# Attention and two feed-forward layers in one kernel: a planner's cost figures, 285 ranks and the place of three steps are changed

## The chip, the cores and the metric

One core of one Trainium2 chip. The metric is the device time of one execution in microseconds (us), median of three runs.

## The reference

Inputs: q, k, v of 4 batches x 8 heads x 576 tokens x 64, a scalar tau, and two pairs of float32 weights (512 x 2048 and 2048 x 512).

```python
scores = q @ k.T / sqrt(64)                        # per batch and head
scores = where(scores >= scores.max(-1) - tau, scores, -1e9)
attn   = exp(scores - scores.max(-1))
x      = (attn / (attn.sum(-1) + 1e-9)) @ v        # -> 2304 tokens x 512
h = x @ moe_w_in;   g = h * sigmoid(1.702 * h);     x = g @ moe_w_out
h = x @ moe2_w_in;  g = h * tanh(softplus(h));      out = g @ moe2_w_out
```

## The kernel before, in words

**Attention.** Heads are taken in pairs (16 of them). A pair of heads gives four full query tiles of 128 rows, and every second pair a mixed tile of the rows left over: 72 tiles in all, called groups in the code. For each group TensorE (PE) makes the scores of two heads into four PSUM banks (`qk`, L591). VectorE (DVE) scales them and takes the row minimum of the negated scores (L614), GpSimd (POOL) adds tau to that minimum (L618), ScalarE (ACT) takes the exponential (L621), DVE masks it and sums the rows (L624). PE then turns the result in 128x128 blocks (`turn`, L660 and L665), ACT copies the turned blocks out (L680), PE multiplies by v (`product`, L703, and `product_mix`, L728) and ACT copies that product out (L712, L735). Only the four banks `sc` hold scores, so the scores of a group wait for the two L614 of the group before.

**Feed-forward layers.** Each layer goes over 3 blocks of 768 tokens and 8 pairs of 128 hidden columns, so there are 24 steps n per layer and 48 in all. `hidden(n)` multiplies by w_in in a 7-product Strassen form (42 matmuls of 384 columns, L829) with ACT and DVE combining and activating (L843, L846, L851), and `out1`/`out2` multiply by w_out (L904, L907, L949). Every float32 matmul is made of three passes over a rounded operand and its remainder (L444/L445, L466/L467, L519/L520).

**Weights.** They arrive as 64-bit words. `conv_w` turns 1024 columns of them into float32: two ACT instructions (L377, L379), two DVE tensor_scalar (L383, L386), one integer addition on POOL (L389), one DVE instruction (L391). `stage` converts the two halves of one pair and stores them to a DRAM tensor `w_d`. `weights(n)` converts on the spot (`stage`, ring `sv` of four tiles), or loads what is in `w_d` back (L427), and then splits it into the operands of step n (L444 to L467). For n of 1 and 2 the operands' tiles share memory with tiles of the attention and open only when that has let go of them. The tuple `EARLY = (1, 2, 3)` says that pairs 0, 1 and 2 are converted during the attention: pair 0 by `weights(0)`, pairs 1 and 2 by `stage` through a ring `sg` of two tiles, to be read back from `w_d` later. `load_xs(0)` brings the attention's output in for block 0 (L494, L520, L524).

**What sets the order.** Nothing is ordered by hand. `Order.add` records every step with its engine, a duration in us, the keys that it reads and writes, and a rank. `Order.run` plays the steps through a list scheduler: an engine that is free takes the ready step of lowest rank and never idles while one is ready; the order that comes out is the order in which the instructions are issued, and on the chip each engine then keeps to it. Attention steps have ranks about equal to their group's number (0 to 71), `load_xs(0)` has 80, all weight work and all feed-forward steps have 5,000 or more. So weight work goes where the plan has an engine free. The durations are formulas (`t_mm`, `t_dve`, `t_act`, `t_tt`), the delay from one engine's end to another's start is the table `LAT`, and steps marked `port` (two-input or fast DVE steps and the POOL steps) may not overlap one another in the plan.

Of the kernel before, what the change touches and what calls it, by code (L numbers as in the profile page):

```python
# [32 lines left out]
FI = 20  # L33
HALF = 384
NHS = 4
SLACK = 0.0
AHEAD = 2
NSS = 6
EARLY = (1, 2, 3)
XR = 80  # L40
S0 = 8
S1 = 2
SR = 0.0
WR = 0.0


class Order:
# [7 lines left out]

    LAT = {
        "PE": {"PE": 0.0, "ACT": 0.27, "DVE": 0.2, "POOL": 0.27, "SP": 0.2},
        "DVE": {"PE": 0.26, "ACT": 0.13, "DVE": 0.13, "POOL": 0.16, "SP": 0.2},
        "ACT": {"PE": 0.22, "ACT": 0.08, "DVE": 0.15, "POOL": 0.16, "SP": 0.2},
        "POOL": {"PE": 0.22, "ACT": 0.08, "DVE": 0.15, "POOL": 0.1, "SP": 0.2},  # L60
        "SP": {"PE": 0.95, "ACT": 0.95, "DVE": 0.95, "POOL": 0.95, "SP": 0.95},
# [2 lines left out]
    def __init__(self):  # L64
        self.ops = []
        self.writer = {}
        self.readers = {}
        self.fill = None
        self.port = set()
        self.mode = {}  # L70

    def add(self, eng, dur, fn, r=(), w=(), rank=0.0, deps=(), nbytes=None, port=False, steps=1, mode=0):
        n = len(self.ops)
        if mode:
            self.mode[n] = mode
        if port:
            self.port.add(n)
        before = set(deps)
        for key in r:
            if key in self.writer:  # L80
                before.add(self.writer[key])
        for key in w:
            if key in self.writer:
                before.add(self.writer[key])
            before.update(self.readers.get(key, ()))
        for key in r:
            self.readers.setdefault(key, []).append(n)
        for key in w:
            self.writer[key] = n
            self.readers[key] = []  # L90
        before.discard(n)
        self.ops.append((eng, dur, fn, before, rank, nbytes, steps))
        return n

    def run(self):
        n_ops = len(self.ops)
        after = [[] for _ in range(n_ops)]
        left = [len(o[3]) for o in self.ops]
        ready = [0.0] * n_ops
        for i, o in enumerate(self.ops):  # L100
            for d in o[3]:
                after[d].append(i)
        engines = sorted({o[0] for o in self.ops})
        free = dict.fromkeys(engines, 0.0)
        future = {e: [] for e in engines}
        now = {e: [] for e in engines}
        for i, o in enumerate(self.ops):
            if not left[i]:
                heapq.heappush(future[o[0]], (0.0, i))
        free["SP"] = 1.0  # L110
        self.last = 0.0
        wire = 0.0
        order = []
        port, done = 0.0, 0
        held, took = 0, {}
        while done < n_ops:
            best = None
            for e in engines:
                if now[e]:
                    t = free[e]  # L120
                elif future[e]:
                    t = max(free[e], future[e][0][0])
                else:
                    continue
                if best is None or t < best[0]:
                    best = (t, e)
            t, e = best
            while future[e] and future[e][0][0] <= t:
                i = heapq.heappop(future[e])[1]
                heapq.heappush(now[e], (self.ops[i][4], i))  # L130
            aside = []
            i = None
            if e == "PE":
                item = min(now[e], key=lambda x: (x[0] + KEEP * (self.mode.get(x[1], 0) != held), x[1]))
                now[e].remove(item)
                heapq.heapify(now[e])
                i = item[1]
            while i is None and now[e]:
                item = heapq.heappop(now[e])
                if item[1] in self.port and port > t + 1e-6:  # L140
                    aside.append(item)
                    continue
                i = item[1]
                break
            for item in aside:
                heapq.heappush(now[e], item)
            if i is None:
                free[e] = port
                continue
            done += 1  # L150
            _, dur, _, _, _, nbytes, _ = self.ops[i]
            if e == "PE" and self.mode.get(i, 0) != held:
                held = self.mode.get(i, 0)
                dur += TURN
            took[i] = dur
            free[e] = end = t + dur
            if i in self.port:
                port = end
            self.last = max(self.last, end)
            if nbytes is not None:  # L160
                wire = end = max(wire, end + DMA_US) + nbytes / DMA_RATE
            order.append((t, i))
            for a in after[i]:
                lat = self.LAT[e][self.ops[a][0]] if dur or nbytes else 0.0
                ready[a] = max(ready[a], end + lat + SLACK)
                left[a] -= 1
                if not left[a]:
                    heapq.heappush(future[self.ops[a][0]], (ready[a], a))
        self.order = order = sorted(order)
        if self.fill is not None:  # L170
            eng, until, dur, fn = self.fill
            at, gaps = 1.2, []
            for t, i in order:
                if i == until:
                    break
                if self.ops[i][0] == eng:
                    n = int((t - at - FG) / dur) if gaps else FI
                    if n > 0:
                        gaps.append((at, i, n))
                    at = t + took[i]  # L180
            order = sorted([(t, i, 0) for t, i in order] + gaps)
        else:
            order = [(t, i, 0) for t, i in order]
        events = []
        for t, i, n in order:
            _, _, fn, *_, steps = self.ops[i]
            dur = took[i]
            if n:
                events.append((t, len(events), self.fill[3], n))
            elif steps == 1:  # L190
                events.append((t, len(events), fn))
            else:
                for k in range(steps):
                    events.append((t + dur * (k + 1) / steps, len(events), next_of, i, k))
        running = {}
        for _, _, fn, *args in sorted(events, key=lambda x: x[:2]):
            if fn is next_of:
                i, k = args
                if k == 0:
                    running[i] = self.ops[i][2]()  # L200
                next(running[i], None)
            else:
                fn(*args)
# [7 lines left out]
def attention_then_two_ffn_kernel(  # L211
# [86 lines left out]
    def t_mm(n, k=1):  # L298
        return k * (max(n, 256) * 0.4167e-3 + 0.0125)
# [8 lines left out]
        return 0.16 + n * 0.97e-3  # L308

    def t_tt(n):  # L310
        return 0.15 + n * 2.1e-3

    def dma(fn, nbytes, r=(), w=(), rank=0.0, deps=(), dur=0.47):
        return add("SP", dur, fn, r, w, rank, deps, nbytes)
# [253 lines left out]
    def qk(tl, rank):  # L568
# [6 lines left out]
        def mm():  # L575
# [18 lines left out]
                yield  # L594

        add("PE", 1.02, mm, [h[2] for h in kqt], [("sc", i) for i in range(4)], rank,
            steps=4 if full else 10, mode=1)
        return [(sc[i][:, :, 0:SH], [("sc", 2 * i), ("sc", 2 * i + 1)]) for i in range(2)]

    def softmax_a(sums, ksum, col, rank, bank, pair, i):  # L600
# [87 lines left out]
    def product(tl, rank):  # L688
# [4 lines left out]
        pn = [p for p, _ in turned[b, hp]]  # L693
        i = avn[0] % 2
        avn[0] += 1
        av, kav = tb[3][:, i * 256:i * 256 + 256], ("tb", 3, i)

        def mm(cs):
            for c in cs:
# [15 lines left out]
    def product_mix(b, hp, i, pn, rank):  # L715

        _, vr, _, kvr = head[b, hp]
        av, kav = tb[2][:, 256 + 64 * i:320 + 64 * i], ("tb", 2, 1 + i)

        def mm():  # L720
            for c in range(5):
# [75 lines left out]
        reopen("g", i, [("p", i)] + ([("pmt", i)] if i < 2 else []))  # L797
    for i in range(3):
        reopen("x2", i, [("vr", i)])
    open_hb = add("SP", 0.0, open_h, deps=scored, rank=-10.0)  # L800
    load_xs(0, XR)
    for n, at in enumerate(EARLY):
# [12 lines left out]
    def hidden(n, rank):  # L815
# [16 lines left out]
                    yield  # L832

        def product(p, dst, kd, start):
            i = add("PE", t_mm(HALF, 6) + 0.03, lambda: mm(p, dst, start),
                    [("xq", p), ("win", n % 3, p)], [kd], rank + PO[p] / 8, [open_hb] if n == 0 else [], steps=6)
            firsts.setdefault(n, i)

        def h(i, j, x, kx, y=None, ky=None):
            ht, kh = hs[i]  # L840
            cs = slice(j * HALF, (j + 1) * HALF)
            if y is not None:
                add("DVE", t_dve(HALF), lambda: nc.vector.tensor_tensor(ht[:, cs], x(), y, ALU.add),  # L843
                    [kx, ky], [kh + (j,)], rank - 4.0)
            add("ACT", t_act(HALF),
                lambda: nc.scalar.activation(ht[:, cs], x() if y is None else ht[:, cs], fn),  # L846
                [kx] if y is None else [], [kh + (j,)], rank - 4.0)

# [86 lines left out]
    def out2(n, rank):  # L935
# [6 lines left out]
        for q, (i, ts) in enumerate(order):  # L942
            g, kg = units[i]

            def mm(i=i, ts=ts, g=g):
# [7 lines left out]
                        )  # L953
                        yield

            add("PE", 3 * len(ts) * t_mm(512), mm, kg + [("wout", n % 3)], [ka2[t] for t in ts],
                rank + (q + 0.5) / len(order), steps=3 * len(ts))
        if k == KP - 1:
            for t in range(6):
# [82 lines left out]
```

## Time and profile before

| what | value |
|---|---|
| median of 3 runs | 1037.9 us (1037.72 to 1038.08) |
| profiled execution | 1037.93 us, of which the span of instructions is 1036.2 us |
| PE, DVE, ACT, POOL busy | 1020.9, 832.7, 659.7, 168.7 us |
| attention, first score to last product | about 6 to 279 us |
| first and second feed-forward layer | about 270 to 655 us, 655 to 1036 us |

The span is the time from the first instruction to the last; 1.7 us of the execution lie around it. A busy PE is one with a matmul under way, and since matmuls are pipelined and long, PE reads as nearly full even where its matmuls start late. DVE and ACT busy times can be taken as they stand. "Idle before" names what ended an engine's idle time. Times are from the start of the span.

### The profile page before, as it was taken

What the parts mean: (1) busy time and instruction counts of PE and PEld (TensorE: products, weight loads), DVE (VectorE), ACT (ScalarE), POOL (GpSimd) and SP (SyncE); (2) the same over time, 40 slices, a digit from 0 to 9 for tenths busy, and PEclk for the clock granted to TensorE, in tenths of its full rate; (3) what the DMA queues carried; (4) which work ended last, traced back from release to release, by engine and by line L of the source; (5) the groups of instructions that cost most, each with busy time, mean ns of one, the idle gap of its engine ahead of it and who ended that gap; (6) DMA issues with size and microseconds to landing.
All of it is one profiled execution on the core that took longest, in us unless ns stands there. A gap on an engine that the chain in (4) does not pass through costs nothing.

```text
span 1036.2 us, 17403 instructions
## 1 busy us (share of the span) xinstructions
PE 1020.9 (99%) x6348; PEld 866.9 (84%) x6348; DVE 832.7 (80%) x1642; ACT 659.7 (64%) x1261; POOL 168.7 (16%) x182
## 2 busy tenths in 40 slices
PE   9999999999999999999999999999999999999998
PEld 6666666666698999999999999988889889889887
DVE  7999999999877889888798888865688665975633
ACT  5988787887866668666687667744464444544421
POOL 2543543333122210111211112000000000000000
PEclk9999999999999999999999999999999999999999
DMA  5434556443145536756376534612125112142001
GB/s 196 126 143 160 175 188 196 131 131 94 45 131 182 180 122 236 250 170 222 134 264 219 203 107 164 199 64 79 63 90 173 62 61 82 46 138 82 21 1 61
DMA packets 55942, 139.62 MB, mean 135 GB/s; under 512 B 8496, under 2 KB 18736, under 8 KB 55856
## 3 DMA queue, kind: packets, MB, share of 16 engines
q1 hardware_dynamic: 55856, 138.51, 39.8%
q8 instruction: 49, 0.80, 0.3%
q14 instruction: 37, 0.30, 0.1%
HBM read 107.48 MB, written 31.01 MB: 134 GB/s over the span
## 4 chain that ended last, share of the span: by engine, by line
PE 80%; ACT 8%; DVE 7%; DMA 2%; issue 1%; POOL 1%; SPq 0%; DVEq 0%; ACTq 0%; POOLq 0%
PE h L829 27%; PE tb L949 13%; PE tb L904 8%; PE sc L591 7%; PE tb L703 7%; PE h L949 6%; PE tb L665 6%; PE h L907 4%; DMA sv<-w_d 1%; PE tb L728 1%; DVE hs L843 1%; DVE xq L520 1%; ACT wout1a L680 1%; ACT sr L379 1%; ACT hs L846 1%
## 5 line engine op out<-in xcount | busy, mean ns | idle before, releaser
L843 DVE TENSOR_TENSOR hs<-h,u 128x384 f32<-128x384 f32 x144 | 79.7, 553 | 78.1 <-ACT u L851 54.5
L829 PE MATMUL h<-xq,win 128*128 128x384 f32 x672 | 131.5, 336 | 2.4 <-ACT u L851 2.2
L829 PE MATMUL h<-xq,win2b 128*128 128x384 f32 x672 | 131.7, 335 | 1.9 <-DVE hs L843 1.5
L829 PE MATMUL h<-xq,win1b 128*128 128x384 f32 x672 | 131.4, 335 | 0.0
L846 ACT ACTIVATE hs<-hs 128x384 f32<-128x384 f32 x144 | 75.9, 527 | 78.9 <-DVE hs L843 77.6
L829 PEld LDWEIGHTS h<-xq,win2b 128*128 128x128 f32 x672 | 116.0, 188 | 8.4 <-DVE hs L843 1.8
L829 PEld LDWEIGHTS h<-xq,win 128*128 128x128 f32 x672 | 115.6, 188 | 8.4 <-ACT u L851 2.9
L829 PEld LDWEIGHTS h<-xq,win1b 128*128 128x128 f32 x672 | 115.9, 188 | 5.6
L851 ACT COPY u<-h 128x384 f32<-128x384 f32 x144 | 68.6, 476 | 78.5 <-PE h L829 78.1
L614 DVE TENSOR_SCALAR_CACHE_REDUCE win2a<-sc,nqsc 128x576 f32<-128x576 f32 x144 | 111.4, 810 | 4.4 <-PE sc L591 4.0
L618 POOL TENSOR_SCALAR nm<-nm,tau_p 128x1 f32<-128x1 f32 x144 | 86.1, 599 | 159.6 <-DVE win2a L614 158.3
L591 PE MATMUL sc<-win1a 64*128 64x288 f32 (+3 forms) x672 | 91.8, 414 | 0.8 <-DVE win2a L614 0.7
L389 POOL TENSOR_TENSOR sg<-sg,sr 128x1024 uint32<-128x1024 uint32 x20 | 51.9, 2594 | 226.7 <-DVE sg L386 225.2
L449 DVE TENSOR_TENSOR sv<-sv 128x256 f32<-128x256 f32 x192 | 84.1, 442 | 0.2
L591 PEld LDWEIGHTS sc<-win1a 64*128 64x128 f32 (+1 forms) x672 | 52.2, 173 | 28.3 <-DVE win2a L614 9.4
L444 ACT CAST win2b<-sv 128x256 fp32r<-128x256 f32 (+1 forms) x96 | 41.9, 442 | 33.6 <-DVE sv L449 28.1
L444 ACT CAST win<-sv 128x256 fp32r<-128x256 f32 (+1 forms) x96 | 42.2, 448 | 30.2 <-DVE sv L449 26.6
L444 ACT CAST win1b<-sv 128x256 fp32r<-128x256 f32 (+1 forms) x96 | 42.1, 444 | 29.4 <-DVE sv L449 23.6
L445 DVE TENSOR_TENSOR win<-sv,win 128x256 fp32r<-128x256 f32 (+1 forms) x96 | 48.9, 512 | 9.7 <-ACT win L444 9.5
L445 DVE TENSOR_TENSOR win2b<-sv,win2b 128x256 fp32r<-128x256 f32 (+1 forms) x96 | 45.9, 479 | 13.5 <-ACT win2b L444 13.4
L445 DVE TENSOR_TENSOR win1b<-sv,win1b 128x256 fp32r<-128x256 f32 (+1 forms) x96 | 44.1, 462 | 11.9 <-ACT win1b L444 11.7
L680 ACT COPY wout1a<-tb 128x512 f32<-128x512 f32 x72 | 40.7, 598 | 11.6 <-PE tb L665 11.3
(242 smaller groups left out, 2283.7 us busy)
## 6 DMA issues: line engine op xcount, KB each, us to landing
sv<-w_d SPq DMA_DIRECT2D x84, 512.0 KB
sr<-in_w_in SPq DMA_DIRECT2D x16, 1024.0 KB
sr<-in_w_out SPq DMA_DIRECT2D x32, 512.0 KB
w_d<-sg SPq DMA_DIRECT2D x20, 512.0 KB
win1a<-in_kq SPq DMA_DIRECT2D x16, 576.0 KB
xr<-x_d SPq DMA_DIRECT2D x24, 384.0 KB
w_d<-sv SPq DMA_DIRECT2D x12, 512.0 KB
x_d<-xo SPq DMA_DIRECT2D x16, 288.0 KB
```

The costliest lines, as they stand in the source:

```text
L444: add("ACT", t_act(256 * m, psum=False), lambda: nc.scalar.copy(at(0), src), [ku] + pre_in, keys, rank)
L445: add("DVE", t_dve(256 * m), lambda: nc.vector.tensor_tensor(at(1), src, at(0), ALU.subtract), [ku], keys, rank, port=True)
L449: add("DVE", t_dve(256), lambda: nc.vector.tensor_tensor(out, x, y, op), [], [ku], rank, port=True)
L591: nc.tensor.matmul(sc[i][at:at + m, g, c0:c0 + n], kq2[rows, q0:q0 + m], kq2[rows, k0:k0 + n], start=True, stop=True)
L614: lambda: nc.vector.tensor_scalar(n3, s3, nqsc, None, ALU.mult, ALU.min, accum_out=nm[:, 0:1]),
L618: lambda: nc.gpsimd.tensor_scalar(nm[:, 1:2], nm[:, 0:1], tau_p, 0.0, ALU.add, ALU.add),
L703: nc.tensor.matmul(av[64 * i:64 * i + 64], vr[:, vc:vc + 64], p[:, a:a + 256], start=(c == 0), stop=(c == 4))
L829: nc.tensor.matmul(dst(), w[:, h, c], xq[p][:, x, cs], start=(start and i == 0), stop=(p in (5, 6) and i == 5), skip_group_check=True)
L843: add("DVE", t_dve(HALF), lambda: nc.vector.tensor_tensor(ht[:, cs], x(), y, ALU.add), [kx, ky], [kh + (j,)], rank - 4.0)
L846: lambda: nc.scalar.activation(ht[:, cs], x() if y is None else ht[:, cs], fn),
L904: nc.tensor.matmul(acc2[e](), w[:, x], g(y)[:, 0:512], start=first, stop=last, skip_group_check=True)
L949: nc.tensor.matmul(acc2[t](), g(x)[:, t * 128:(t + 1) * 128], w[:, y], start=(k == i == j == 0), stop=(k == KP - 1 and i == 1 and j == 2), ...
```

## The change

1. `EARLY` becomes `(1,)`: pairs 1 and 2 are no longer converted through `sg` and read back; `weights(1)` and `weights(2)` now call `stage` themselves, through `sv`, as pairs 3 to 7 did.
2. A ScalarE activation with the Gelu function on the [128, 1] tile `nqsc` is added. It writes the key `qsc`, which L618 and L624 read, so it comes after the last L624 of the attention; its rank is 1,000.
3. The planner's figures change: DVE to DVE delay 0.13 to 0, DVE to POOL 0.16 to 0.24, POOL's addition 2.1 to 2.25 ns per column, the matmul groups 0.024 us shorter (L829) or 0.0057 us a matmul longer (L949); the scores' consumers may be planned 0.1 us before the end of the scores (`soon`); POOL steps of up to 0.5 us no longer take the port; on a tie POOL is served first; the first activation of the second layer is planned 1.28 us longer.
4. The two halves of the PSUM bank `tb3` in `product`, and the parts of `tb2` in `product_mix`, get the key of the whole bank, so that the plan has one wait for the other.
5. The ranks of 285 steps, attention and feed-forward, are shifted by whole numbers of eighths, between -168/8 and 165/8 (table `NUDGE`, by the step's number).

What is computed stays the same.

```diff
-SLACK = 0.0
-EARLY = (1, 2, 3)
+EARLY = (1,)
+GR = 1e3
+NUDGE = {
+    14: 7, 26: -2, 43: 53, 54: -34, 59: -17, 67: -3, 70: -1, 80: -3, 86: -5, 87: -32, 116: 49, 121:
...
+    4278: 2,
+}
-        "DVE": {"PE": 0.26, "ACT": 0.13, "DVE": 0.13, "POOL": 0.16, "SP": 0.2},
+        "DVE": {"PE": 0.26, "ACT": 0.13, "DVE": 0.0, "POOL": 0.24, "SP": 0.2},
...
+        rank += NUDGE.get(n, 0) / 8
         self.ops.append((eng, dur, fn, before, rank, nbytes, steps))
...
-                if best is None or t < best[0]:
+                if best is None or t < best[0] or t == best[0] and e == "POOL":
...
-            if i in self.port:
+            if i in self.port and (e != "POOL" or dur > 0.5):
                 port = end
...
-                ready[a] = max(ready[a], end + lat + SLACK)
+                ready[a] = max(ready[a], end + lat - self.soon.get(i, 0.0))
...
     def t_tt(n):
-        return 0.15 + n * 2.1e-3
+        return 0.15 + n * 2.25e-3
...
-            steps=4 if full else 10, mode=1)
+            steps=4 if full else 10, mode=1, soon=0.1)
...
-        av, kav = tb[3][:, i * 256:i * 256 + 256], ("tb", 3, i)
+        av, kav = tb[3][:, i * 256:i * 256 + 256], ("tb", 3)
...
-        av, kav = tb[2][:, 256 + 64 * i:320 + 64 * i], ("tb", 2, 1 + i)
+        av, kav = tb[2][:, 256 + 64 * i:320 + 64 * i], ("tb", 2)
...
+    add("ACT", 1.5, lambda: nc.scalar.activation(nqsc, nqsc, AF.Gelu_apprx_sigmoid), w=["qsc"], rank=GR)
     open_hb = add("SP", 0.0, open_h, deps=scored, rank=-10.0)
...
-            i = add("PE", t_mm(HALF, 6) + 0.03, lambda: mm(p, dst, start),
+            i = add("PE", t_mm(HALF, 6) + 0.006, lambda: mm(p, dst, start),
...
-            add("ACT", t_act(HALF),
+            add("ACT", t_act(HALF) + (1.28 if n == NPAIR and (i, j) == (0, 0) else 0.0),
...
-            add("PE", 3 * len(ts) * t_mm(512), mm, kg + [("wout", n % 3)], [ka2[t] for t in ts],
+            add("PE", 3 * len(ts) * (t_mm(512) + 0.0057), mm, kg + [("wout", n % 3)], [ka2[t] for t in ts],
```

## Rows read from the trace of the kernel before

**Rows 1.** The page, busy time of two engines: us, share of span, instructions.
```profile
PE 1020.9 (99%) x6348; PEld 866.9 (84%) x6348; DVE 832.7 (80%) x1642; ACT 659.7 (64%) x1261; POOL 168.7 (16%) x182
```

**Rows 2.** Busy time by stretch: length, then each engine, clock, DMA share, GB/s.
```profile
25.00:250.00 225.00, 220.76 (x1934) 145.13 (x1932) 223.31 (x563) 186.17 (x370) 91.82 (x129) 1.00 0.47 151
272.00:330.00 58.00, 54.01 (x348) 49.41 (x347) 43.44 (x66) 41.11 (x73) 12.51 (x5) 1.00 0.39 126
330.00:1030.00 700.00, 699.07 (x3736) 639.35 (x3735) 526.28 (x890) 399.68 (x758) 54.20 (x21) 1.00 0.38 130
```

**Rows 3.** Chain that ended last: start, us, work; first score, then a mixed group's.
```profile
5.84 1.22 PE sc L591 x8
...
49.08 0.73 PE tb L728 x20
...
50.95 1.17 PE sc L591 x8
52.12 1.02 PE tb L665 x8
53.15 0.11 PE tb L660
```

**Rows 4.** The same chain, end of the attention: v product, early feed-forward matmuls.
```profile
266.43 2.31 PE tb L703 x20
...
269.88 1.05 PE h L829 x6
...
274.92 2.11 PE h L829 x12
```

**Rows 5.** Timeline of PE from 278 us: start, us, line; last products, first waits.
```profile
278.43 0.34 PE L728 MATMUL tb<-wout2a,x20a 128*64 128x64 f32 x4 [0.31 <-ACT xo L735]
278.59 0.29 PE L728 MATMUL tb<-g1a,x20a 128*64 128x64 f32 x4
278.81 2.36 PE L829 MATMUL h<-xq,win 128*128 128x384 f32 x12
283.32 0.97 PE L829 MATMUL h<-xq,win 128*128 128x384 f32 x4 [2.16 <-ACT u L851]
```

**Rows 6.** DVE's groups by line, 0 to 272 us: count | busy us, mean ns.
```profile
L614 DVE TENSOR_SCALAR_CACHE_REDUCE win2a<-sc,nqsc 128x576 f32<-128x576 f32 x144 | 111.4, 810 | 4.4 <-PE sc L591 4.0
L391 DVE SCALAR_TENSOR_TENSOR sg<-sr,sg 128x1024 uint32<-128x1024 uint32 x4 | 4.9, 1216 | 0.0
L383 DVE TENSOR_SCALAR sg<-sg 128x1024 f32<-128x1024 f32 x4 | 2.7, 680 | 0.0
L386 DVE TENSOR_SCALAR sg<-sg 128x1024 uint32<-128x1024 uint32 x4 | 2.7, 675 | 0.0
```

**Rows 7.** Mask-and-sum on one of four tiles, to 270 us: ns min/median/max.
```profile
L624 DVE SCALAR_TENSOR_TENSOR g2a<-win2a,nm,g2a x36: 779/812/1765, 15.0 to 267.6; 128x577 f32<-128x577 f32 x36
```

**Rows 8.** Timeline of POOL and DVE about 105 to 110 us.
```profile
105.59 0.80 DVE L624 SCALAR_TENSOR_TENSOR g2a<-win2a,nm,g2a 128x577 f32<-128x577 f32 x1
105.09 0.29 POOL L618 TENSOR_SCALAR nm<-nm,tau_p 128x1 f32<-128x1 f32 x1 [1.57 <-DVE win2a L614]
105.83 0.72 POOL L618 TENSOR_SCALAR nm<-nm,tau_p 128x1 f32<-128x1 f32 x1 [0.45 <-DVE win2a L614]
107.80 2.41 POOL L389 TENSOR_TENSOR sg<-sg,sr 128x1024 uint32<-128x1024 uint32 x1 [1.25 <-DVE sg L386]
109.05 1.78 DVE L624 SCALAR_TENSOR_TENSOR g3a<-win2a,nm,g3a 128x577 f32<-128x577 f32 x1
```

**Rows 9.** Timeline of ACT at the first Gelu.
```profile
278.16 0.21 ACT L735 COPY xo<-tb 128x64 f32<-128x64 f32 x1 [0.25 <-PE tb L728]
278.39 1.28 ACT L846 ACT_TABLE_LOAD   x1
279.69 0.53 ACT L846 ACTIVATE hs<-hs 128x384 f32<-128x384 f32 x1
```

**Rows 10.** DVE's groups by line, 272 to 330 us: the conversions of pairs 3 on.
```profile
L391 DVE SCALAR_TENSOR_TENSOR sv<-sr,sv 128x1024 uint32<-128x1024 uint32 x5 | 8.3, 1669 | 4.9 <-POOL sv L389 4.9
```

More of the change, by code (lines that the diff above doesn't have):

```diff
@@ L70, in __init__, with add @@
         self.mode = {}
-    def add(self, eng, dur, fn, r=(), w=(), rank=0.0, deps=(), nbytes=None, port=False, steps=1, mode=0):
+        self.soon = {}
+    def add(self, eng, dur, fn, r=(), w=(), rank=0.0, deps=(), nbytes=None, port=False, steps=1, mode=0, soon=0.0):
         n = len(self.ops)
@@ L77, in add @@
             self.port.add(n)
+        if soon:
+            self.soon[n] = soon
         before = set(deps)
```

28 rows, old and new, of the table NUDGE are left out of this document.

## The prediction, made blind

> **What bounds the kernel now.** I read the page's busy times first, then busy time by stretch, then the chain of waits, then DVE's groups. The page has PE at 99% [rows 1], and that figure misleads: it counts a matmul as long as it is under way. The stretches are more telling [rows 2]. From 330 to 1030 us PE is idle for 700 - 699.07 = 0.9 us in all, with DVE at 75% and ACT at 57%; both feed-forward layers run at PE's own pace, and no order of steps can take anything there. From 272 to 330 us PE is idle for 58 - 54.01 = 4.0 us. From 25 to 250 us, the attention, DVE is busy 223.31 of 225 us: it never stands still.
>
> How much PE waits in the attention is read from the chain, whose pieces give what a matmul group takes when it runs on without a wait. A full group costs PE 1.17 (scores) + 1.02 + 0.11 (turning) + half of 2.31 (product with v, made for two groups at once) = 3.455 us; a mixed one 1.17 + 1.13 + 2 x 0.73 = 3.76 us [rows 3, 4]. 64 full and 8 mixed groups are 221.1 + 30.1 = 251.2 us. PE's attention goes from the first score at 5.84 [rows 3] to 278.81 [rows 5], 273.0 us, of which 1.05 + 2.11 = 3.2 us are feed-forward matmuls already placed there [rows 4]. That leaves 269.8 us for 251.2 us of work: **PE waits 18.6 us inside the attention.** So the whole kernel has about 18.6 + 4.0 + 0.9 = 23.5 us that a better order could reach, and 18.6 of them lie where DVE is full.
>
> **The change part by part.**
>
> *EARLY.* Of each conversion DVE pays 4.9/4 + 2.7/4 + 2.7/4 = 2.58 us, and four of them (pairs 1 and 2, through `sg`) lie in the attention: 10.3 us [rows 6]. POOL's addition costs DVE more than that: while L389 ran from 107.80 to 110.21, an L624 that began at 109.05 took 1.78 us [rows 8] against a median of 0.81 [rows 7]. Four such holds are at most 4 x 0.97 = 3.9 us. If all four conversions leave the attention, DVE is relieved of 14.2 us; if all stay, of nothing. Both are possible, since the conversions are no less needed and still have a rank under everything else: the planner puts them wherever it has DVE free. Pair 1's has two free `sv` tiles from the start, so it can be placed as before; pair 2's must wait for the two tiles that pair 0's split gives back. I take half, **-7.1 us**, with 0 and -14.2 as ends. The four loads back from `w_d` (512 KB each) go and nothing replaces them; DMA is under half used there [rows 2], so I price them at nothing. Stores to `w_d` remain, as later blocks read them.
>
> The conversions that leave return between 272 and 330 us. Five lie there now, and the DVE part L391 takes 1.67 us on average instead of 1.22 [rows 10, 6], since POOL's addition and the small splits meet. PE's idle time there beyond the 2.16 us discussed below is 4.0 - 2.2 = 1.8 us, or 0.37 us a conversion. Two more: **+0.7 us**. The ends: 0, as DVE has 58 - 43.4 = 14.6 us free [rows 2], and 2 x (1.67 + 0.68 + 0.68) = +6.1 us if PE pays for all their DVE time.
>
> *The added Gelu.* Between the attention and the first activation ACT loads its table, 1.28 us from 278.39, with the activation right behind it at 279.69 [rows 9]. That was on the chain, and PE then stood 2.16 us for ACT's copy L851 [rows 5]. After the change the load happens once the last L624 is through. It still takes ACT's time, now beside PE work on the last groups, where a turned block may come out later by as much: the cover is the products, and without them nothing is won. I take **-1.3 us**; the ends are 0 and -2.2.
> The Trainium skill ("ScalarE: Activation LUTs", What ACT_TABLE_LOAD costs) puts a switch at about 2.66 us, a drain of 1.38 us beside the load. By that the sum below would come out 1.4 us lower. The rows show no drain: 0.02 us lie between the copy's end and the load, and 0.02 us between the load and the activation [rows 9].
>
> *Planner's figures, bank keys and ranks.* These add no instruction; they alter which ready step an engine takes. The first Gelu aside, the bank keys match what the chip does: the second `product_mix` waited 0.31 us for ACT to copy a neighbouring part of the same bank [rows 5], and the old plan did not know it. DVE's own idle time from 25 to 250 us is 1.7 us [rows 2] and one more hold like that in rows 8 is 1.0 us, for pair 0's conversions stay in the attention. That a plan closer to the chip saves: **-2.7 us**. The ends are 0, or a loss as in the third rival, and -(18.6 - 7.1) = -11.5 us, PE's whole remaining wait.
>
> *After 330 us.* Nothing, with an end of -0.9 and one of +4.0, what the stretch ahead of it loses now.
>
> **Sum:** -7.1 + 0.7 - 1.3 - 2.7 = -10.4 us. The profiled execution took 1037.93 us (span 1036.2), the median of the runs is 1037.9, so both lead to **1027.5 us**.
>
> **The rivals.**
>
> *1. PE becomes the bound of the attention.* All of DVE's relief arrives, the corrected plan keeps DVE and PE fed, and most of the 18.6 us goes. For it: 14.2 us of relief and DVE's other waits together reach nearly that sum, and PE's floor is far enough below. Against it: in 72 groups each handing over four times, some wait is left. With three quarters of the 18.6 us or all of it, and the 1.3 to 2.2 us of the table: 1037.9 - 15.3 = 1022.6 down to 1017.1, say 1019.
>
> *2. The order on the chip does not follow the plan, or fills the same gaps with the same steps.* The conversions stay as filling, DVE remains full, and shifted ranks pay off only in the plan. For it: no rank of weight work can fall among the attention's ranks, so the same work is ready in the same gaps. Against it: four of the six conversions in the attention had been asked for by `EARLY`. What is left is the table load: 1036.6, or 1037.9 if even that only moves.
>
> *3. Slower: the weights of step 2 come late.* If pair 2's conversions slip to the end of the attention while the attention does not get shorter, because the scores of one group wait for the two L614 of the last and not for DVE's total, then step 1's splits, step 2's conversions and the first activations queue on DVE between 272 and about 302 us. A conversion is a series over ACT, DVE, POOL, DVE, and whatever stands behind L391 on DVE (sums L843, which PE waits for) stands as long. It decides when DVE's 14.6 free microseconds are not spread but lie behind PE's need. Price: the +6.1 us end, with nothing won in the attention and the table's 1.3 us lost in the same queue: 1044.0.
>
> *4. Small POOL steps hold DVE.* The new plan lets L618 lie under two-input DVE steps. If each such overlap held L624 as L389 does, one in eight of 144 at 0.29 us [rows 8] would cost 5.2 us: 1032.7. The rows speak against it: L618 took 0.29 us alone and 0.72 us beside an L624 that kept its 0.80 us, so it is POOL that waits [rows 8], and L624's median is 0.81 us [rows 7].
> The Trainium skill ("SBUF — State Buffer", SBUF: two separate sides) states an exclusive lock for the whole instruction in favour of whichever starts first, which would let a small POOL step hold DVE too. The trace agrees for L389; for L618 it shows only the DVE side holding.
>
> **How the numbers follow.** My forecast, roughly 1022 to 1034, has 0.50; rival 1 has 0.20, rival 2 has 0.12, rival 3 has 0.13, rival 4 has 0.05. The range should leave out 2 in 10: rival 3 and the lowest part of rival 1 stay out. The lower end is all waits and the whole 2.2 us less some: 1037.9 - 21.7 = 1016. The upper end takes in rival 2 with a little noise: 1038.5. A run can tell about 0.2%, or 2.1 us, from no change. Faster by more than that is the forecast, rival 1, rival 4 and a share of rival 2: 0.76. Within it is most of rival 2: 0.10. Slower is rival 3 and a little of rival 2: 0.14.
>
> **What would show each step.** Right: fewer than six L391 before the last score, or the same number with fewer L624 above 1 us; the last product on PE near 268 instead of 279 us with the same floor of 251 us; the table load at some point before the last product and the 2.16 us wait gone; PE idle in the 58 us behind the attention's end between 3 and 4.5 us; after that no more than 1 us of idle PE. Wrong: an attention as long as before with DVE still full (rival 2); an attention with DVE idle (rival 1, and then PE's waits name the next bound); PE waiting for L843 or for the splits L445 of steps 1 and 2 (rival 3). If the feed-forward layers after 330 us change by more than 2 us, I have missed a mechanism.

## The result and the profile after

The changed kernel takes **1026.52 us** (median of 4 runs, 1026.13 to 1027.34) against 1037.99 us (4 runs, 1037.72 to 1038.66) of the kernel before beside it: ratio 0.9886, 95% interval 0.9873 to 0.9900. The prediction was 1027.5 us. The total was right; of the four terms of the sum behind it the two large ones were wrong, in opposite directions, so that their errors cancelled.

The stretches of the changed kernel, by engine (columns as in [rows 2]); the last two of them lie 11 us earlier than their counterparts, as the kernel does:

```profile
25.00:250.00 225.00, 224.30 (x1972) 147.17 (x1972) 222.39 (x568) 188.82 (x377) 91.88 (x132) 1.00 0.42 137
262.00:320.00 58.00, 58.00 (x385) 52.45 (x383) 50.10 (x91) 45.78 (x84) 11.38 (x6) 1.00 0.48 155
319.00:639.00 320.00, 320.00 (x1846) 299.51 (x1845) 274.91 (x429) 230.34 (x412) 58.30 (x22) 1.00 0.55 189
639.00:1019.00 380.00, 380.00 (x1904) 341.53 (x1903) 254.82 (x462) 171.36 (x349) 0.00 (x0) 1.00 0.25 83
```

And the two counterparts of the last two in the kernel before:

```profile
330.00:650.00 320.00, 319.16 (x1836) 297.77 (x1835) 275.98 (x432) 227.50 (x410) 54.20 (x21) 1.00 0.55 190
650.00:1030.00 380.00, 379.91 (x1902) 341.57 (x1901) 250.30 (x459) 172.17 (x349) 0.00 (x0) 1.00 0.24 80
```

Three things are to be seen. In the same 225 us of the attention PE runs 38 matmuls more than before (1972 against 1934) while DVE is as full as it was (222.4 against 223.3 us of 225 [rows 2]). In the 58 us behind the attention PE's 4.0 us of idle time [rows 2] are gone. And in the first feed-forward layer, which had looked full, PE runs 1846 matmuls in 320 us instead of 1836; at 320/1846 = 0.173 us each that is 1.7 us. The counts may be compared, since both traces hold the same 6312 matmuls behind the start-up ones (36 of L542 before, 50 of L579 now).

The end of the attention, from the chain that ended last, and PE's timeline of the last product:

```profile
5.89 1.48 PE sc L628 x8
...
265.90 1.05 PE h L867 x6
...
270.39 2.11 PE h L867 x12
272.50 0.73 PE tb L765 x20
273.24 2.29 PE h L867 x12
275.52 0.73 PE tb L765 x20
276.26 4.40 PE h L867 x24
```
```profile
275.97 0.29 PE L765 MATMUL tb<-g1a,x20a 128*64 128x64 f32 x4
276.19 2.36 PE L867 MATMUL h<-xq,win 128*128 128x384 f32 x12
```

By the prediction's own count the attention now takes 276.19 - 5.89 = 270.3 us less 1.05 + 2.11 + 2.29 = 5.45 us of feed-forward matmuls inside it: 264.9 us, where it took 269.8. So the 11.2 us by which the span fell (1036.2 to 1025.0) are **4.9 us in the attention, 4.0 us in the 58 us behind it, 1.7 us in the first feed-forward layer**, and less than a microsecond elsewhere; 0.3 of the 4.0 us is the wait ahead of the last product [rows 5], which the 4.9 us hold too. The chain that ended last says the same in one line of the page (by engine; before, PE had 80% of it and ACT and DVE 15%):

```profile
PE 97%; DVE 1%; ACT 1%; issue 0%; POOL 0%; POOLq 0%; DVEq 0%; ACTq 0%
```

The prediction expected conversions to leave the attention. They did not; DVE's groups up to its last mask hold all six, now all in `sv`. One thing did leave, block 1's four multiplications: eight lay ahead of the last mask before, four do now. The line of the kernel before (0 to 272 us, last mask at 270.0), then two of the changed kernel (0 to 266 us, last mask at 265.2):

```profile
L494 DVE TENSOR_TENSOR xr<-xr,rb 128x768 f32<-128x768 f32 x8 | 7.6, 950 | 0.0
```
```profile
L428 DVE SCALAR_TENSOR_TENSOR sv<-sr,sv 128x1024 uint32<-128x1024 uint32 x6 | 7.3, 1214 | 0.0
L531 DVE TENSOR_TENSOR xr<-xr,rb 128x768 f32<-128x768 f32 x4 | 3.8, 938 | 0.0
```

That is 3.8 us less DVE work in the attention, which the prediction had not looked for. It does not explain the gain by itself: when the same four are moved out in the kernel before (`e10_before_x_late` below), the attention gets longer.

### The profile page after: what moved, and what is told of

Same layout as the page of the kernel before. It is cut to its first block, busy times and chain, and to the rows that moved or that the text cites. A ratio compares the mean times of both kernels' runs of the same rounds, so it can differ in the third digit from the quotient of the medians.

```text
span 1025.0 us, 17308 instructions
## 1 busy us (share of the span) xinstructions
PE 1018.3 (99%) x6362; PEld 866.5 (85%) x6362; DVE 831.7 (81%) x1642; ACT 660.0 (64%) x1262; POOL 170.2 (17%) x182
## 4 chain that ended last, share of the span: by engine, by line
PE 97%; DVE 1%; ACT 1%; issue 0%; POOL 0%; POOLq 0%; DVEq 0%; ACTq 0%
PE h L867 34%; PE tb L987 13%; PE tb L942 13%; PE sc L628 8%; PE tb L740 7%; PE h L945 7%; PE h L987 6%; PE tb L702 6%; PE tb L697 1%; PE tb L765 1%; PE tb L579 1%; DVE win2a L651 0%; ACT wout1a L717 0%; ACT g2a L658 0%; DVE g0a L661 0%
## 5 line engine op out<-in xcount | busy, mean ns | idle before, releaser
L881 DVE TENSOR_TENSOR hs<-h,u 128x384 f32<-128x384 f32 x144 | 79.8, 554 | 88.9 <-PE h L867 55.6
L655 POOL TENSOR_SCALAR nm<-nm,tau_p 128x1 f32<-128x1 f32 x144 | 84.2, 586 | 159.8 <-DVE win2a L651 156.5
L486 DVE TENSOR_TENSOR sv<-sv 128x256 f32<-128x256 f32 x192 | 80.3, 419 | 1.3
L426 POOL TENSOR_TENSOR sg<-sg,sr 128x1024 uint32<-128x1024 uint32 x16 | 42.5, 2655 | 215.0 <-DVE sg L423 125.1
L482 DVE TENSOR_TENSOR win<-sv,win 128x256 fp32r<-128x256 f32 (+1 forms) x96 | 50.6, 532 | 10.4 <-ACT win L481 10.4
L426 POOL TENSOR_TENSOR sv<-sv,sr 128x1024 uint32<-128x1024 uint32 x16 | 43.0, 2685 | 79.0 <-DVE sv L423 44.7
L482 DVE TENSOR_TENSOR win1b<-sv,win1b 128x256 fp32r<-128x256 f32 (+1 forms) x96 | 48.2, 506 | 7.5 <-ACT win1b L481 7.3
```

The costliest lines, as they stand in the source:

```text
L426: lambda: nc.gpsimd.tensor_tensor(bits, bits, word(0), ALU.add), keys, [kval], rank, port=True)
L482: add("DVE", t_dve(256 * m), lambda: nc.vector.tensor_tensor(at(1), src, at(0), ALU.subtract), [ku], keys, rank, port=True)
L486: add("DVE", t_dve(256), lambda: nc.vector.tensor_tensor(out, x, y, op), [], [ku], rank, port=True)
L655: lambda: nc.gpsimd.tensor_scalar(nm[:, 1:2], nm[:, 0:1], tau_p, 0.0, ALU.add, ALU.add),
```

## The experiments

Each run is compared with the kernel before on the same chip. "Last mask" is the start of the last L624 (L661 in the changed kernel), read from one trace of each run. The changed kernel, the run with the copy and the run with the attention's shifts alone differ little in the attention and lie within 0.7 us there, so less than that is no difference.

| run | us | ratio to before, 95% interval | last mask at | PE idle 265 to 325 us |
|---|---|---|---|---|
| kernel before | 1038.0 | 1 | 270.0 | 4.0 |
| changed kernel | 1026.5 | 0.9886 (0.9873 to 0.9900) | 265.2 | 0.0 |
| no rank shifts | 1036.5 | 0.9983 (0.9973 to 0.9994) | 268.5 | 1.3 |
| shifts of the attention alone | 1032.6 | 0.9947 (0.9931 to 0.9964) | 264.7 | 0.6 |
| shifts of the feed-forward steps alone | 1032.5 | 0.9948 (0.9934 to 0.9963) | 268.0 | 0.7 |
| shifts with the old figures and keys | 1053.6 | 1.0150 (1.0126 to 1.0173) | 279.1 | 1.6 |
| figures and keys alone | 1037.8 | 0.9995 (0.9986 to 1.0005) | 269.6 | 2.3 |
| EARLY alone | 1040.0 | 1.0010 (1.0001 to 1.0020) | 272.5 | 2.3 |
| copy in place of the Gelu | 1027.3 | 0.9892 (0.9877 to 0.9907) | 264.6 | 0.7 |

**Which part gives the time: no rank shifts** (`e1_no_nudge`).

```diff
-        rank += NUDGE.get(n, 0) / 8
+        rank += 0.0
```

> The changed kernel with the 285 rank shifts left out (all else kept). Theory 'the ranks': the shifts give most of the 11.5 us, since the conversions stayed in the attention and DVE is as full as before; then 1034 to 1039 us, with PE waits of over 15 us in the attention and 3 us or more of idle PE in the 60 us behind it. Rival 'the figures': the corrected durations, delays and keys alone make a better order and the shifts add 3 us at most; then 1027 to 1030 us.

Measured 1036.5 us, ratio 0.9983. Everything in the change but the shifts is worth 0.17%, about 1.8 us; the shifts are worth the other 1%. The theory of the ranks held; which of the 285 shifts do it was not tested further than the two halves below. Its figures for the waits were too high for the second place (PE idles 1.3 us, not 3, from 265 to 325 us).

**Figures and keys alone** (`e5_figures_keys`): the changed kernel without shifts, with `EARLY = (1, 2, 3)` and without the added Gelu.

> The kernel before with the planner's new figures and bank keys alone: EARLY as before, no added Gelu, no rank shifts. Theory 'the ranks': 1035 to 1040 us, the same pitch of the score groups (3.65 us) as before. Rival 'the figures': 1028 to 1031 us, pitch near 3.6 us.

Ratio 0.9995, no difference that the runs can tell. Correcting the planner did not by itself give a better order.

**The shifts on the old figures** (`e9_old_figures`): the changed kernel with all edits of durations, delays, rules and keys taken back.

```diff
-        "DVE": {"PE": 0.26, "ACT": 0.13, "DVE": 0.0, "POOL": 0.24, "SP": 0.2},
+        "DVE": {"PE": 0.26, "ACT": 0.13, "DVE": 0.13, "POOL": 0.16, "SP": 0.2},
-            if i in self.port and (e != "POOL" or dur > 0.5):
+            if i in self.port:
-            steps=4 if full else 10, mode=1, soon=0.1)
+            steps=4 if full else 10, mode=1)
...
```

> The changed kernel with its 285 rank shifts, EARLY and the added Gelu, but with the planner's durations, delays, port rule, tie rule and bank keys as they were before. Theory 'the shifts are fitted to the corrected plan': they give little or harm here, 1035 to 1045 us. Rival 'the shifts are a better order by themselves': 1026 to 1030 us.

1053.6 us, 1.5% slower than before, the last mask 14 us later than in the changed kernel:

```profile
L661 DVE SCALAR_TENSOR_TENSOR g3a<-win2a,nm,g3a x36: 778/816/823, 19.9 to 279.1; 128x577 f32<-128x577 f32 x36
```

Part of this is the clock. PE waited 1.66 and 2.37 us for DVE's minima, and its granted clock then averaged 0.57 from 15 to 19 us and 0.62 from 35 to 39.5 us, where the changed kernel had 1.00. The shifts are no better order by themselves: the plan that they were made for is another one with the other figures. Which steps they then put wrong was not followed. So the corrected figures matter only together with the shifts: alone 0, shifts without them +1.5%, both -1.1%.

**Where the shifts act** (`e6_nudge_att`, `e7_nudge_ffn`).

```diff
-        rank += NUDGE.get(n, 0) / 8
+        rank += (NUDGE.get(n, 0) / 8 if n < 1401 else 0.0)     # or: if n >= 1401
```

> The changed kernel with the rank shifts of the attention's steps alone. Theory 'the gain is two separate gains, attention 4 us and feed-forward 5 us, each from its own shifts': last L624 near 265 us as in the changed kernel, but PE's losses behind the attention near 10 us as without shifts; 1031 to 1033 us. Rival 'the feed-forward layers follow from an attention that ends well': 1027 to 1029 us.

> The changed kernel with the rank shifts of the feed-forward steps alone. Theory 'two separate gains': attention as without shifts (last L624 near 268.5 us), PE's losses behind it down from 10.9 to about 6 us; 1031 to 1033 us. Rival 'the shifts work only together, being fitted to one plan': 1036 to 1040 us.

1032.6 and 1032.5 us: two separate gains, each about 0.36% (3.7 us) below the kernel without shifts, and together 1%. That this is more than the sum of the two, 0.7%, lies within the intervals. The traces place them. First the run with the attention's shifts, then the one with the feed-forward shifts:

```profile
25.00:250.00 225.00, 224.31 (x1975) 147.51 (x1972) 222.55 (x568) 188.49 (x378) 91.77 (x131) 1.00 0.42 137
265.00:325.00 60.00, 59.36 (x382) 54.38 (x381) 54.06 (x87) 46.04 (x82) 13.26 (x6) 1.00 0.50 156
330.00:650.00 320.00, 317.86 (x1824) 297.48 (x1823) 272.28 (x427) 227.43 (x406) 51.99 (x20) 0.99 0.55 188
```
```profile
25.00:250.00 225.00, 222.65 (x1944) 148.16 (x1940) 222.01 (x561) 187.34 (x372) 83.73 (x129) 1.00 0.45 140
265.00:325.00 60.00, 59.28 (x391) 53.02 (x390) 48.27 (x86) 47.43 (x87) 13.53 (x8) 1.00 0.40 129
330.00:650.00 320.00, 319.89 (x1844) 299.15 (x1844) 267.05 (x429) 229.49 (x409) 53.18 (x20) 1.00 0.56 193
```

With the attention's shifts PE runs 1975 matmuls in 225 us, as the changed kernel does; with the others 1944, as the kernel without shifts does (1944 there too). From 330 to 650 us it is the other way round: 1824 with the attention's shifts, 1844 with the others, 1831 without any. In the first of these PE waits 2.1 us for one of DVE's sums (L881) near 391 us, and its granted clock averages 0.57 from 394 to 398 us; that costs time as well.

**EARLY alone** (`e4_before_early`).

```diff
-EARLY = (1, 2, 3)
+EARLY = (1,)
```

> The kernel before with EARLY = (1,) alone. Theory of the prediction (pair 2's conversions leave the attention, DVE is relieved): 1030 to 1033 us, fewer than six L391 before the last score. Theory read from the changed kernel's trace (the conversions stay as filling, six of them before 200 us): 1036 to 1040 us, six L391 in the attention.

1040.0 us, ratio 1.0010 (1.0001 to 1.0020): no gain, and if anything a loss of 1 us. That loss goes with the clock: where the mean granted clock was 1.000, in two runs of ten, the time was 1037.6 us, and at 0.997 or 0.998 it was 1039.3 to 1041.3 us. Six conversions lay before 150 us, as in the kernel before. The four loads back from DRAM that the edit saves were worth nothing, as the prediction had it; the relief of DVE did not take place.

**What if the conversions do leave** (`e8_conv_late`): pairs 1 and 2 held until the last group's masks.

```diff
-    weights(1, BIG + 1 + WR)
+    weights(1, BIG + 1 + WR, [marks[-1]])
-            weights(n + 2, rank + WR)
+            weights(n + 2, rank + WR, [marks[-1]] if n == 0 else [])
```

> The changed kernel with the conversions of pairs 1 and 2 held until the last group's masks are done: the step that the prediction priced at -7.1 us for half of it. It takes 4 x 2.6 = 10.3 us of DVE work out of the attention and puts it behind. Theory 'DVE's total sets the attention': the last L624 comes 8 to 12 us earlier (253 to 257 us), and PE then waits in the 60 us behind; the total is 1024 to 1032 us. Rival 'PE's and ACT's handing over sets the attention': last L624 at most 4 us earlier (261 us or later), DVE idle by 6 us or more, and a total of 1032 to 1042 us.

1057.0 us, 1.8% slower than before (ratio 1.0179, 1.0163 to 1.0194). The attention did not get shorter (last mask at 266.4, against 265.2 us) although DVE now stood idle for 8.4 of 225 us in it:

```profile
25.00:250.00 225.00, 224.15 (x1965) 146.99 (x1965) 216.63 (x560) 182.22 (x369) 71.19 (x127) 1.00 0.34 106
265.00:325.00 60.00, 47.12 (x271) 39.95 (x270) 44.04 (x60) 37.32 (x64) 15.77 (x6) 0.83 0.57 184
```

PE ran 1965 matmuls in the 225 us, seven fewer than in the changed kernel. The place of the conversions did not stay empty: block 1's four multiplications, 3.8 us, came back ahead of the last mask, and still DVE stood idle. Behind the attention PE stood for 12.9 of 60 us, and the granted clock averaged 0.83 over that stretch, so that part of its work went at the lower level, 1.2 GHz instead of 2.4. The waits of that stretch name the split of step 1:

```profile
PE h L867 <- ACT win1b L481: 5.2, 1, 5.2
PE h L867 <- DVE win1b L482: 3.7, 2, 3.3
```

This includes the loads of the words, which also began only then, and their 7.8 us of DVE idle time. The rival was right on the attention; on the total both missed by 15 us or more: neither had priced a series of load, ACT, DVE, POOL and DVE standing ahead of steps 1 and 2 with no attention left to cover it.

**Block 1's multiplications held back** (`e10_before_x_late`), on the kernel before: the loads of block 1's activations wait for the last group's masks.

> The kernel before with the loads of block 1's activations held until the last group's masks, so that its four multiplications (L494, 0.87 us each) leave the attention; nothing else is changed but what the planner makes of it. Theory 'DVE's total sets the attention': last L624 3 to 4 us earlier, near 266.5 us, total 1034 to 1036 us. Rival 'another step fills the gap': last L624 within 1.5 us of 270 us, total 1037 to 1039 us.

1045.4 us, ratio 1.0070 (1.0055 to 1.0085), last mask at 271.9 us. The four L494 left, and the attention became 1.8 us longer. Both totals expected were too low, and neither the theory nor the rival held: no step filled the gap, since DVE was idle for 5.0 of the 225 us from 25 to 250, and still nothing was won. From 330 to 650 us PE ran 1807 matmuls where the kernel before ran 1836, 29 x 0.173 = 5.0 us behind. Half of the PE waits that the trace names from 280 to 650 us are for DVE's sums (L843): 3.7 us, against 1.7 us in the kernel before.

**Lighter work in the same order.** Three runs keep every instruction's place and only shorten some, by leaving out part of six conversions, part of the v products, or both. DVE lighter (`e11_dve_light`):

```diff
-            lambda: nc.vector.tensor_scalar(val, val, cmin, cmax, ALU.max, ALU.min),
+            lambda: nc.vector.tensor_scalar(val[:, 0:c], val[:, 0:c], cmin, cmax, ALU.max, ALU.min),
...
```

> The changed kernel, order of all instructions kept, with the three DVE instructions of the first six conversions working on 64 of 1024 columns (the weights of pairs 0 to 2 of the first layer are left unconverted in the other columns): about 13 us less DVE work in the attention, PE's work as it was. Theory 'PE's own work with its handovers sets the attention': last L661 at most 4 us earlier than 265.2 us, DVE idle by 9 us or more. Rival 'DVE's total sets it' (the prediction's reading): 9 to 13 us earlier, 252 to 256 us. Third, 'each of the two is a bound with the other close behind': 3 to 6 us earlier.

PE lighter (`e12_pe_light`), in `product`:

```diff
                 for i in range(2):
+                    if c == 1:
+                        yield
+                        continue
```

> The changed kernel, order of all other instructions kept, with the second of the five chunks of every v product of the full groups left out (4 of 20 matmuls, 0.46 of 2.31 us, in 32 products): 14.8 us less PE work in the attention, DVE's as it was. Theory 'PE's own work sets the attention': last L661 9 to 14 us earlier, 251 to 256 us. Rival 'DVE's total sets it': at most 3 us earlier, 262 us or later. Third, 'both close': 3 to 6 us earlier.

Both (`e13_both_light`):

> Both of the last two together: the three DVE instructions of the first six conversions on 64 columns and one of five chunks of the v products left out. Theory 'PE sets it': as with PE's alone, within 2 us. Rival 'DVE sets it': as with DVE's alone, within 2 us. Third, 'both close': more than the sum of the two alone, 9 us or more earlier than 265.2 us.

One execution each: 1027.7, 1023.3 and 1021.6 us, against 1026.5 us; the last mask at 266.1, 262.4 and 260.7 us, against 265.2. From 25 to 240 us, in the order changed kernel, DVE lighter, PE lighter, both:

```profile
25.00:240.00 215.00, 214.30 (x1866) 140.29 (x1867) 212.57 (x544) 180.34 (x360) 87.97 (x126) 1.00 0.42 136
```
```profile
25.00:240.00 215.00, 213.78 (x1861) 139.74 (x1861) 202.66 (x543) 179.55 (x360) 79.40 (x126) 1.00 0.42 136
```
```profile
25.00:240.00 215.00, 212.22 (x1799) 139.15 (x1799) 214.06 (x550) 183.07 (x365) 89.25 (x128) 1.00 0.43 138
```
```profile
25.00:240.00 215.00, 212.21 (x1828) 138.79 (x1825) 206.76 (x554) 182.82 (x366) 80.13 (x127) 1.00 0.44 141
```

Relieving DVE gives nothing: it idles for 12.3 us instead of 2.4, and the last mask comes 0.9 us later. So DVE, full as it is, does not set the attention. What it waits for now is PE's scores (25 to 240 us; the changed kernel first, then DVE lighter, whose line numbers are 4 higher):

```profile
DVE win2a L651 <- PE sc L628: 1.0, 4, 0.3
```
```profile
DVE win2a L655 <- PE sc L632: 7.9, 12, 1.3
```

Taking some 14 us from PE (32 products of 2.31 us, which take 1.88 with 16 matmuls instead of 20) gives 2.8 us, so PE's total does not set it either; in that run PE's weight loads wait longer for DVE's minima (25 to 240 us; the changed kernel first, then PE lighter):

```profile
PEld sc L628 <- DVE win2a L651: 5.2, 16, 0.4
```
```profile
PEld sc L628 <- DVE win2a L651: 15.0, 39, 0.9
```

Whichever of the two is relieved waits for the other where the scores are handed over. With both lighter only 4.5 us come, half of the least that "both close" had expected, though DVE's relief is then worth 1.7 us instead of nothing. Part of DVE's relief was also spent on POOL: in the run with DVE lighter one mask that began during an addition took 2.96 us, where the longest in the changed kernel took 2.09. What is left is the order itself: in a sequence laid out for steps of full length, a shortened step mostly turns into waiting for the next hand-over. That is a reading and not shown; which hand-over closes the ring was not settled.

**The added Gelu** (`e2_copy`).

```diff
-    add("ACT", 1.5, lambda: nc.scalar.activation(nqsc, nqsc, AF.Gelu_apprx_sigmoid), w=["qsc"], rank=GR)
+    add("ACT", 1.5, lambda: nc.scalar.copy(nqsc, nqsc), w=["qsc"], rank=GR)
```

> The changed kernel, the added Gelu on the [128, 1] tile replaced by a plain copy, so that the order of all instructions stays and only the place of the table load moves back to the first activation. Theory 'the load was on the path': 1.3 to 2.2 us slower than the changed kernel, 1027.8 to 1028.7 us. Rival 'the new order has slack there': no difference over 0.5 us, 1026.0 to 1027.0 us.

Ratio 0.9892 (0.9877 to 0.9907) against 0.9886 of the changed kernel: the intervals cover each other, so the run times show no difference. The trace shows a small cost between the two expectations. ACT with the copy, and PE behind it; below, ACT of the changed kernel:

```profile
273.19 1.28 ACT L884 ACT_TABLE_LOAD   x1
```
```profile
278.62 2.35 PE L867 MATMUL h<-xq,win1b 128*128 128x384 f32 x12 [0.53 <-ACT hs L884]
```
```profile
266.60 1.28 ACT L837 ACT_TABLE_LOAD   x1
267.89 0.20 ACT L837 ACTIVATE nqsc<-nqsc 128x1 f32<-128x1 f32 x1
268.00 0.57 ACT L717 COPY wout2a<-tb 128x512 f32<-128x512 f32 x1
```

In the new order the load stands where PE has other matmuls, and without the Gelu PE loses 0.7 us from 265 to 325 us, not the 2.2 us of before.

## Why the prediction was right, and where it was right for the wrong reason

**The total** (-10.4 us forecast, -11.2 us of span measured) and the side were right, but the total by luck. The prediction put 7.1 + 2.7 = 9.8 of its 10.4 us into the attention, where 4.9 came, and 0.6 us behind it, where over 6 came. Its own sign for the attention was a last product near 268 us; it ended at 276.2 us. For the 58 us behind the attention it had expected PE to idle for 3 to 4.5 us; it idles for none. The other signs came true: six L391 (now L428) as before, with four masks above 1 us instead of five; the table load lies ahead of the last product, the 2.16 us wait is gone, and after 320 us PE is never idle by busy time.

**EARLY, -7.1 us: wrong.** The step was "If all four conversions leave the attention, DVE is relieved of 14.2 us", and half of that was taken. None left, and the edit alone measured 1.0010. The rule that weight work fills what the plan leaves free, which the prediction itself gave as the other end, decided. The deeper error was to turn DVE's relief into time one for one, because DVE "never stands still": a full DVE was read as the bound. With 9.9 us less of DVE's busy time in the same order the attention did not shorten. DVE's 99% holds work that the planner put into gaps; the six conversions alone are 15.5 us of it (7.3 us in L428 and 8.2 us in the two steps ahead of it).

**Conversions returning, +0.7 us, and rival 3.** None returned, so the term was 0. When they were made to leave, the price was far over rival 3's +6.1 us: from 1026.5 to 1057.0 us, with the loads' start and a lower clock in it. Rival 3's mechanism exists; the change did not go there. Its reason, that the scores wait for the two L614 of the group before and not for DVE's total, is what the runs with lighter work support; it would have been the better ground for the first term.

**The added Gelu, -1.3 us: the mechanism right, the size half.** 0.7 us of PE's idle time in the trace, inside the bounds of 0 and -2.2. The prediction priced it in the old order, where the load stood on the chain; in the new one other work covers most of it. Nothing of a drain beside the 1.28 us is seen here either: the Gelu starts 0.01 us behind the load.

**Figures, keys and ranks, -2.7 us: the term that was mis-sized.** It was priced by what DVE's 1.7 us of idle time and one hold would give, which follows from the same wrong reading. The shifts alone are worth 1% (0.9983 to 0.9886), 10 us, in two halves: attention and feed-forward steps. The end of -11.5 us that the prediction kept for this term was near.

**After 330 us, nothing: wrong by 1.7 us.** "PE is idle for 700 - 699.07 = 0.9 us in all" was read from busy time, the very figure whose fault the first paragraph names. The count of matmuls in equal stretches shows what it hid: 1836 against 1846 in 320 us.

**Rival 1** did not come true: no relief of DVE came, the attention still takes 264.9 us for PE's 251.2, and although the chain is now 97% PE, some 14 us less PE work won only 2.8 us. **Rival 2** is what the change without its shifts did (0.9983). **Rival 4:** the small POOL steps hold nothing. 55 of the 144 masks began while one of them (L655) was under way, and the longest of these took 0.83 us; on the tile whose L661 met no addition the longest took 0.82 us:

```profile
L661 DVE SCALAR_TENSOR_TENSOR g2a<-win2a,nm,g2a x36: 807/815/822, 15.9 to 261.4; 128x577 f32<-128x577 f32 x36
```

## What to carry to other kernels

An engine that a list scheduler fills can be 99% busy without being the bound, as DVE was here: shorten its work in the unchanged order and see whether the end moves. In this kernel, whose engines run in a fixed order, a better planner model gained nothing by itself and the same rank shifts on the old model lost 1.5%; model and search had to be judged together, and the fitted table was of use only to its own plan. For an engine whose instructions overlap, count instructions in equal stretches of the same kind of work instead of adding busy time; check first that both traces hold them all.

## What the runs showed that was not expected

Moving four conversions (10.3 us of DVE) from inside the attention to behind it cost 30 us, three times their own time, with their loads begun later as well and PE's granted clock down to a mean of 0.83 there. Behind the load of ACT's table PE waited 2.2 us in one order and 0.5 us in another. And six conversions cut from 15.5 to 3.6 us on DVE together with some 14 us less work on PE, in an unchanged order, shortened the attention by 4.5 us.
